# Two DVE operations for each weight tile, new planned durations and priorities in a fused attention and mixing kernel

## The chip, the cores and the metric

The kernel runs on one core of one Trainium2 chip. The metric is the device time of one execution in microseconds. Three runs of the kernel before took 783.48, 783.9 and 786.11 us (median 783.9).

The engines are named as in the profile: PE (TensorE, matmuls; PEld is its weight load), DVE (VectorE), ACT (ScalarE), POOL (GpSimd), SP (SyncE, whose queue issues all DMAs here). Each engine takes its instructions in order.

## The reference

Queries, keys and values have shape (4 batches, 8 heads, 576 positions, 64). Three steps follow each other:

```python
# 1. attention, the sum of two branches
q_d, k_d, v_d = means over groups of 4 positions          # 144 positions
out_up    = repeat(softmax(q_d k_d^T / 8) v_d, 4)
out_local = softmax(q k^T / 8 where |i - j| < 4) v
x = (out_up + out_local) as (4, 576, 512)
# 2. channel mixing with the row before
xk = mu_k * x + (1 - mu_k) * x_prev
xr = mu_r * x + (1 - mu_r) * x_prev
x  = sigmoid(xr @ w_r) * (relu(xk @ w_k)**2 @ w_v)
# 3. normalisation and a two-layer block
x  = x + relu(layernorm(x) * g_ln @ w_ch1) @ w_ch2
```

w_r is 512 x 512, w_k 512 x 1024, w_v 1024 x 512, w_ch1 512 x 2048, w_ch2 2048 x 512. These five weights arrive as 64-bit floats, everything else as 32-bit floats.

## The kernel before, in words

**Attention** is done in 16 units, one for each pair of heads and batch (units 0 to 3 are batch 0). A unit loads its keys, queries and values, brings keys and queries to a layout with the head dimension on partitions, forms the banded scores (`score`, L584) and the scores of the means (`dscore`, L614), takes both softmaxes on DVE and ACT, multiplies with the values (`upper` L678, `pvmm` L700) and adds the two branches into a 128-row slice of xT (L725). All four units of a batch are needed for one row block of step 2, because each gives 128 of the 512 channels.

**Forms of the loads.** The parameters m0 to m15 choose for each unit how keys and queries come in (`load`, L459): 0 is four DMAs for each tensor in 128-byte runs and a transpose on DVE (L525); 1 is two DMAs in 256-byte runs and six transposes on PE (L544); 2 is two DMAs in 1536-byte runs and twelve small matmuls with the identity on PE (L538); 3 loads as 1 does and multiplies with a matrix that also gives the sums over four positions (L541). In all forms but 0, ACT or DVE copies the result out of PSUM.

**Steps 2 and 3** run over six chunks of 384 rows. A product in 32-bit precision is three matmuls (`mm3`, L740 to L743): each operand is split into a high and a low part, and high x high, high x low and low x high are added up in PSUM. Step 3 does its first two chunks directly and the last four in pairs by a seven-product scheme (`m2_h`).

**Weights.** `load_split` (L396) takes each of 52 tiles of 128 x 512 weights (4 of w_r, 8 of w_k, 8 of w_v, 16 each of w_ch1 and w_ch2): a DMA of 64-bit words into w64 (two buffers), a conversion to 32-bit floats in wf (two buffers), a copy of the high part, a subtraction for the low part. The conversion (`load_f32`, L371 to L394) is one ACT operation, the absolute value of the high words read as 32-bit floats (L379), and four on DVE: a clamp from below (L382), a shift by 3 with a mask (L385), an OR with the low word's three top bits (L388) and an OR with the sign (L392).

**The order** is worked out by a planner in Python (`Plan`, L61). Every operation is added with an engine (or several to choose from), an assumed duration and a priority; the planner simulates the engines and takes, at each step, the operation that can start earliest, the lowest priority value first among those ready. Its sequence is what is issued, so it fixes the order on each in-order queue. Assumed durations come from `c_act`, `c_dve`, `c_pool` and `c_dma` (L241 to L254) and from constants; DMAs are one engine "SP" that is busy for the assumed transfer time, and their data is taken to land 2.2 us after it. Priorities come from the dictionary `PRM` (L26). `LOAD` adds a handicap to DVE where an operation has a choice.

**Filler.** 40 warm-up matmuls of 128 columns (`warm_up`, L415) go first, four or five ahead of each score of batch 0, and `issue` (L221) adds one for each 0.06 us in which the plan has PE idle, until PSUM bank pv2 is needed.

**Small loads.** mu_k, mu_r and g_ln (512 values each) are loaded into [128, 4] tiles, in 4-byte pieces (L340, L341, L1217).

## Time and profile before

| | |
|---|---|
| runs | 783.48, 783.9, 786.11 us |
| profiled execution, its own time | 791.19 us |
| its span | 789.4 us |
| mean granted TensorE clock | 0.982 |
| PE, PEld busy | 762.4 us (97%), 667.3 us (85%) |
| DVE, ACT, POOL busy | 531.6 us (67%), 374.3 us (47%), 116.1 us (15%) |
| moved by DMA | 120.31 MB in 187,199 packets |

The busy times are averages over stages with different limits, and a PE that is busy with filler counts as busy. In the rows below, a window's line gives for each engine the busy time and in brackets how many instructions ran; PEclk is the granted clock as a share of full speed. A wait's line names the instruction that waited, then what released it. "issue" is time in which an engine waited for nothing that the profile shows.

### The profile page before, as it was taken

The numbers are of one execution on the slowest core, as the hardware profiler recorded it, in microseconds if no ns is written. First come the engines' busy times: TensorE is split into PE (matmuls) and PEld (weight loads), VectorE is DVE, ScalarE is ACT, GpSimd is POOL, SyncE is SP. The second block draws the span as 40 slices with busy tenths as digits, with TensorE's granted clock in tenths as the row PEclk, the third lists the DMA queues.
The fourth block names the chain that finished last, engine by engine and source line by source line (L and its number), as shares of the span: only waits on it lengthen the run. The fifth ranks groups of instructions, "written<-read, shape, count | busy, mean of one in ns | idle before, by whom it ended". The sixth has DMA issues, their size and how long they took to land.

```text
span 789.4 us, 15623 instructions
## 1 busy us (share of the span) xinstructions
PE 762.4 (97%) x5940; PEld 667.3 (85%) x5940; DVE 531.6 (67%) x1094; ACT 374.3 (47%) x854; POOL 116.1 (15%) x162
## 2 busy tenths in 40 slices
PE   7798789999999999999999999999999999999998
PEld 7677667788788798888999999998988888898986
DVE  5799698974775768998889986737553355333233
ACT  4678676765865766858644334411421131111110
POOL 6332243312320100100001022200100030000000
PEclk9789898999999999999999999999999999999999
DMA  8899799453540033446475698887854346544422
GB/s 214 176 165 166 151 174 150 102 97 81 124 52 22 34 119 128 159 149 167 129 190 169 196 328 224 252 321 263 196 152 112 117 121 216 171 120 113 128 68 80
DMA packets 187199, 120.31 MB, mean 152 GB/s; under 512 B 129524, under 2 KB 154996, under 8 KB 187124
## 3 DMA queue, kind: packets, MB, share of 16 engines
q1 hardware_dynamic: 187124, 119.32, 58.8%
q8 instruction: 47, 0.77, 0.4%
q14 instruction: 28, 0.23, 0.1%
HBM read 90.44 MB, written 28.84 MB: 151 GB/s over the span
## 4 chain that ended last, share of the span: by engine, by line
PE 82%; DVE 7%; DMA 5%; ACT 3%; issue 2%; SPq 1%; DVEq 0%; ACTq 0%
PE pso L742 8%; PE pso L743 8%; PE pso L741 8%; PE psh L741 7%; PE psh L743 7%; PE psh L742 7%; PE psk L741 4%; PE psk L743 4%; PE psk L742 4%; PE psv L741 4%; PE psv L742 4%; PE psv L743 4%; PE pv L711 2%; DMA w<-in_moe_w_k_dram 2%; PE ds L619 2%
## 5 line engine op out<-in xcount | busy, mean ns | idle before, releaser
L741 PE MATMUL psh<-xn,sa 128*128 128x384 f32 x224 | 75.7, 338 | 1.8 <-ACT u L359 1.0
L743 PE MATMUL psh<-xn,sa 128*128 128x384 f32 x224 | 75.5, 337 | 0.0
L742 PE MATMUL psh<-xn,sa 128*128 128x384 f32 x224 | 75.3, 336 | 0.0
L741 PEld LDWEIGHTS psh<-xn,sa 128*128 128x128 f32 x224 | 42.1, 188 | 7.0 <-ACT u L359 1.4
L379 ACT ACTIVATE wf<-w 128x512 f32<-128x512 f32 x52 | 34.7, 668 | 27.1 <-DMA w<-in_moe_w_ch_dram 10.2
L742 PEld LDWEIGHTS psh<-xn,sa 128*128 128x128 f32 x224 | 42.1, 188 | 3.9
L743 PEld LDWEIGHTS psh<-xn,sa 128*128 128x128 f32 x224 | 42.1, 188 | 0.0
L367 ACT ACTIVATE c22h<-t 128x384 fp32r<-128x384 f32 x16 | 8.4, 525 | 66.2 <-DVE t L1136 66.2
L367 ACT ACTIVATE kr<-psk 128x384 f32<-128x384 f32 x46 | 22.5, 490 | 34.7 <-PE psk L743 29.0
L388 DVE SCALAR_TENSOR_TENSOR wf<-w,wf 128x512 uint32<-128x512 uint32 x52 | 37.0, 714 | 0.5
L392 DVE SCALAR_TENSOR_TENSOR wf<-w,wf 128x512 uint32<-128x512 uint32 x52 | 36.7, 707 | 0.4
L806 DVE TENSOR_TENSOR kl<-kr,kh 128x384 fp32r<-128x384 f32 x38 | 21.7, 570 | 20.3 <-ACT kr L805 20.1
L382 DVE TENSOR_SCALAR wf<-wf 128x512 f32<-128x512 f32 x52 | 24.1, 464 | 15.8 <-ACT wf L379 15.6
L367 ACT ACTIVATE hh<-psh 128x384 fp32r<-128x384 f32 x32 | 15.7, 489 | 35.9 <-PE psh L743 35.3
L417 PE MATMUL warm<-identb 128*128 128x128 bf16 x308 | 27.6, 244 | 3.9 <-issue 2.1
L572 POOL TENSOR_TENSOR v<-v 72x512 f32<-72x512 f32 x16 | 21.7, 1357 | 57.6 <-DMA v<-in_v_dram 50.0
L417 PEld LDWEIGHTS <-identb 128*128 128x128 bf16 x308 | 22.2, 111 | 5.3 <-issue 2.7
L363 ACT COPY PT<-pT 32x288 f32<-32x288 f32 x54 | 23.1, 428 | 6.8 <-PE pv L711 5.8
L367 ACT ACTIVATE c11h<-psh 128x384 fp32r<-128x384 f32 x16 | 7.9, 491 | 38.6 <-PE psh L743 38.5
L803 ACT ACTIVATE kh<-kr 128x384 fp32r<-128x384 f32 x48 | 25.1, 524 | 0.8
L1113 DVE SCALAR_TENSOR_TENSOR c11l<-psh,c11h 128x384 fp32r<-128x384 f32 x16 | 8.8, 553 | 24.4 <-ACT c11h L367 24.2
L854 POOL TENSOR_TENSOR raw<-raw 128x384 f32<-128x384 f32 x5 | 5.9, 1181 | 128.3 <-DVE xn L1081 67.7
(772 smaller groups left out, 2396.8 us busy)
## 6 DMA issues: line engine op xcount, KB each, us to landing
sa<-s_dram SPq DMA_DIRECT2D x112, 256.0 KB
w<-in_moe_w_ch_dram SPq DMA_DIRECT2D x32, 512.0 KB
s_dram<-s SPq DMA_DIRECT2D x16, 512.0 KB
vw<-in_v_dram SPq DMA_DIRECT2D x62, 96.0 KB
v<-in_v_dram SPq DMA_DIRECT2D x16, 288.0 KB
x_dram<-r SPq DMA_DIRECT2D x18, 256.0 KB
x1t<-x_dram SPq DMA_DIRECT2D x6, 768.0 KB
z_dram<-x1t SPq DMA_DIRECT2D x18, 256.0 KB
```

The lines of the kernel that those rows point to most:

```text
L363: return [("ACT", c_act(n), lambda: nc.scalar.copy(dst(), src()), False), ("DVE", c_dve(n, True), lambda: nc.vector.tensor_copy(dst(), src ...
L367: return [("ACT", c_act(n, True), lambda: nc.scalar.activation(dst(), src(), AF.Relu), False), ("DVE", c_dve(n), lambda: nc.vector.tensor_ ...
L379: add("ACT", c_act(512), prio, lambda: nc.scalar.activation(f(), w64().bitcast(F32)[:, :, 1], AF.Abs), r=[w64], w=[f])
L382: add("DVE", c_dve(512, True), prio, lambda: nc.vector.tensor_scalar_max(f(), f(), TINY), w=[f], port=True)
L388: lambda: nc.vector.scalar_tensor_tensor(fu(), w64()[:, :, 0], 29, fu(), op0=ALU.logical_shift_right, op1=ALU.bitwise_or),
L392: lambda: nc.vector.scalar_tensor_tensor(fu(), w64()[:, :, 1], 0xC0000000, fu(), op0=ALU.bitwise_and, op1=ALU.bitwise_or),
L417: nc.tensor.matmul(warm()[:, :P], identb, identb, start=True, stop=True)
L572: lambda: nc.gpsimd.tensor_tensor(v4()[:, :, 0:2, :], v4()[:, :, 0:2, :], v4()[:, :, 2:4, :], op=ALU.add),
L741: nc.tensor.matmul(ps, lh, rh, start=start, stop=False, skip_group_check=more)
L742: nc.tensor.matmul(ps, lh, rl, start=False, stop=False, skip_group_check=more)
L743: nc.tensor.matmul(ps, ll, rh, start=False, stop=stop, skip_group_check=more)
L803: add("ACT", c_act(C), prio, lambda: nc.scalar.activation(kh(), kr(), AF.Square), r=[kr], w=[kh])
```

## The change

The conversion of a weight tile keeps two DVE operations. The absolute value on ACT now also scales by 2^-112, which puts the exponent where the shift by 3 needs it, so that clamp and mask go; a second ACT operation takes the top byte of each low word and writes it, scaled to 0 to 7, as a 32-bit integer in place, so that the OR needs no shift of its own.

```diff
-            add("ACT", c_act(512), prio, lambda: nc.scalar.activation(f(), w64().bitcast(F32)[:, :, 1], AF.Abs),
-                r=[w64], w=[f])
+            add("ACT", c_act(512), prio, lambda: nc.scalar.activation(
+                f(), w64().bitcast(F32)[:, :, 1], AF.Abs, scale=2.0 ** -112), r=[w64], w=[f])
+            add("ACT", c_act(512), prio, lambda: nc.scalar.activation(
+                w64()[:, :, 0], w64().bitcast(U8).rearrange("p a (b c) -> p a b c", c=4)[:, :, 0, 3], AF.Copy,
+                scale=7.45 / 255), w=[w64])
             fu = lambda: f().bitcast(U32)
-            add("DVE", c_dve(512, True), prio, lambda: nc.vector.tensor_scalar_max(f(), f(), TINY), w=[f],
-                port=True)
-            add("DVE", c_dve(512, True), prio,
-                lambda: nc.vector.tensor_scalar(fu(), fu(), 3, 0x3FFFFFF8, op0=ALU.logical_shift_left,
-                                                op1=ALU.bitwise_and), w=[f], port=True)
             add("DVE", c_dve(512), prio,
-                lambda: nc.vector.scalar_tensor_tensor(fu(), w64()[:, :, 0], 29, fu(),
-                                                       op0=ALU.logical_shift_right, op1=ALU.bitwise_or),
+                lambda: nc.vector.scalar_tensor_tensor(fu(), fu(), 3, w64()[:, :, 0],
+                                                       op0=ALU.logical_shift_left, op1=ALU.bitwise_or),
                 r=[w64], w=[f], port=True)
```

The planner's durations are set anew, and its DMAs now take 0.47 us of SP each and then pass one shared queue:

```diff
 def c_act(n, psum=False, ap=0):
-    return (0.05 if psum else 0.093) + n / 1200 + 0.093 * ap
+    return (0.07 if psum else 0.113) + n / 1200 + 0.093 * ap
 def c_dve(n, fast=False):
-    return 0.066 + n / (1920 if fast else 960)
+    return 0.116 + n / (1920 if fast else 960)
 def c_pool(n):
-    return 0.1 + n * 0.0022
+    return 0.2 + n * 0.0028
-def c_dma(nbytes, small=False):
-    return max(0.41, nbytes / 360e3 * (2 if small else 1))
+def c_dma(nbytes, run=2048):
+    return nbytes / run * min(6.5 + run / 18, 20 + run / 26) / 16e3
...
+            if eng == "SP":
+                free[eng] = at + self.ISSUE
+                moved = max(moved, free[eng]) + cost
+                end = moved + o.lat
```

Constants of single operations change too (the copies into PT are costed as 420 elements instead of 288, `upper` 0.71 instead of 0.6, a matmul triple 3 x 0.0165 over its columns instead of 0.01). Nearly all values of `PRM` change: the handicap of DVE from 0.36 to 0.47; the priority base of w_r from -25.74 to -43.615 with a step for each tile of -56.938 instead of -0.4; the limit on thin matmuls in a row (`thin`) from 7.21 to 14.233; and the forms of the units:

```diff
-m0=2, m1=1, m2=1, m3=1, m4=3, m5=0, m6=1, m7=0, m8=0, m9=0
+m0=2, m1=1, m2=0, m3=3, m4=1, m5=0, m6=0, m7=2, m8=3, m9=0
```

Form 2 loads both heads of a tensor in one DMA instead of two. Filler is 304 columns wide, 17 ahead of all, two ahead of each score of batch 0, one for each 0.14 us of planned idle time:

```diff
-    def warm_up(n=40):
+    isumb = isum.bitcast(BF16)
+    def warm_up(n=17):
         for _ in range(n):
-            nc.tensor.matmul(warm()[:, :P], identb, identb, start=True, stop=True)
+            nc.tensor.matmul(warm()[:, :304], identb, isumb, start=True, stop=True)
...
-    plan.issue(lambda: warm_up(1), 0.06, pvs[0][2])
+    plan.issue(lambda: warm_up(1), 0.14, pvs[0][2])
```

mu_k, mu_r and g_ln are loaded together as rows of 512 bytes and transposed on PE:

```diff
-            add("SP", 0.9, PRM["mu"], load_mu, w=[mub], lat=2.2)
+            raw = Buf(wk, [P, C], F32, "kr", 1, "vraw")
+            for i, src in enumerate((mu_k, mu_r, g_ln)):
+                add("SP", 0.05, PRM["mu"], lambda i=i, src=src: nc.sync.dma_start(
+                    out=raw()[KT * i:KT * i + KT, :P], in_=src.rearrange("(k p) -> k p", p=P)), w=[(raw, i)], lat=2.2)
+            vps = Buf(ps_k, [P, 512], F32, "pk", 2, "vps")
+            add("PE", 0.1, PRM["mu"] + 8.0, lambda: nc.tensor.transpose(
+                vps()[:, :3 * KT], raw()[:3 * KT, :P], ident[:3 * KT, :3 * KT]), r=[raw], w=[vps])
+            add("ACT", c_act(12, True), PRM["mu"] + 8.0, lambda: nc.scalar.copy(vecs, vps()[:, :3 * KT]), r=[vps], w=[mub])
```

The sum of four value rows, two POOL operations before, becomes one step that the planner may give to POOL or, as a single reduction over 1,024 elements, to DVE; the scaling of the maxima by -1/128 may go to ACT instead of DVE.

## Rows read from the trace of the kernel before

**Rows 1.** Windows by stage: busy us and instructions of each engine, TensorE clock, DMA share, GB/s.
```profile
0.00:59.00 59.00, 49.10 (x937) 42.41 (x938) 44.81 (x96) 36.73 (x97) 27.01 (x52) 0.88 0.90 185
59.00:150.00 91.00, 80.17 (x1095) 64.68 (x1093) 79.26 (x169) 65.67 (x167) 27.55 (x39) 0.92 0.89 155
150.00:420.00 270.00, 269.38 (x2112) 234.67 (x2112) 213.33 (x460) 181.67 (x413) 37.01 (x51) 1.00 0.43 112
```

**Rows 2.** Groups by line, engine PE, first 60 us: busy us, mean ns, idle before.
```profile
L417 PE MATMUL warm<-identb 128*128 128x128 bf16 x297 | 25.1, 244 | 3.9 <-issue 2.1 <-DVE identb L318 1.8
```

**Rows 3.** Waits of PE, first 150 us: us in total, times, longest us.
```profile
PE up L681 <- ACT pdT L674: 3.7, 1, 3.7
PE sc L593 <- issue: 3.2, 2, 2.8
PE ds L619 <- DVE e L607: 2.5, 1, 2.5
PE warm L417 <- issue: 2.1, 1, 2.1
```

**Rows 4.** Windows of the four stretches behind those waits, columns as in rows 1.
```profile
22.30:26.50 4.20, 4.20 (x50) 3.50 (x50) 2.21 (x8) 1.05 (x3) 0.81 (x3) 0.50 1.03 198
...
37.80:43.50 5.70, 5.69 (x126) 4.29 (x126) 4.85 (x12) 3.18 (x10) 1.61 (x3) 0.50 1.05 154
...
89.60:95.50 5.90, 5.86 (x33) 4.63 (x34) 4.73 (x11) 3.33 (x8) 1.82 (x2) 0.50 0.70 208
...
119.30:126.50 7.20, 7.20 (x50) 5.42 (x51) 5.22 (x11) 3.69 (x12) 3.35 (x4) 0.53 0.78 128
```

**Rows 5.** DMA queues in the window from 17 to 24 us: packets, MB, share.
```profile
q1 hardware_dynamic: 3070, 1.61, 97.2%
q8 instruction: 1, 0.02, 1.1%
```

**Rows 6.** Chain of waits: start us, us, what; pieces between 28 and 109 us.
```profile
28.97 0.50 PE tq L544 x6
...
65.18 1.39 PE tq L541 x12
...
76.11 0.67 ACT wf L379
...
78.26 7.58 DMA w<-in_moe_w_k_dram
85.93 0.66 ACT wf L379
...
108.05 0.67 ACT wf L379
```

**Rows 7.** Groups by line, whole span: the conversion's operations (x52 weight tiles).
```profile
L379 ACT ACTIVATE wf<-w 128x512 f32<-128x512 f32 x52 | 34.7, 668 | 27.1 <-DMA w<-in_moe_w_ch_dram 10.2 <-DMA w<-in_moe_w_k_dram 8.2 <-DMA w<-in_moe_w_r_dram 6.5
...
L382 DVE TENSOR_SCALAR wf<-wf 128x512 f32<-128x512 f32 x52 | 24.1, 464 | 15.8 <-ACT wf L379 15.6
...
L385 DVE TENSOR_SCALAR wf<-wf 128x512 uint32<-128x512 uint32 x52 | 23.4, 452 | 0.3
```

**Rows 8.** Windows where the chain runs on DVE, lines L382, then L385: DVE busy us.
```profile
103.90:119.20 15.30, 1.62 (x2) 1.00 1.10 201
...
sum 40.80, DVE 2.45; mean DVE 0.82
...
103.90:119.20 15.30, 1.24 (x3) 1.00 1.10 201
...
sum 40.80, DVE 2.49; mean DVE 0.83
```

**Rows 9.** DMA in the window from 9 to 13.5 us: all packets.
```profile
DMA packets 2622, 0.95 MB, mean 211 GB/s; under 512 B 2493, under 2 KB 2493, under 8 KB 2621
```

**Rows 10.** Timeline of PE: start us, us; unit 0's transposes of keys and queries.
```profile
7.93 1.21 PE L538 MATMUL tq<-isum,kin 96*64 96x96 f32 x24
8.97 1.16 PE L538 MATMUL tq<-isum,qin 96*64 96x96 f32 x24
```

More of the change, by code (lines that the diff above doesn't have):

```diff
@@ L13 @@
 U32 = mybir.dt.uint32
+U8 = mybir.dt.uint8
 BF16 = mybir.dt.bfloat16
@@ L61 @@
 class Plan:
-    SYNC = {"PE": 0.2, "ACT": 0.15, "DVE": 0.14, "POOL": 0.16, "SP": 0.0, "CTL": 0.0}
+    SYNC = {"PE": 0.21, "ACT": 0.16, "DVE": 0.14, "POOL": 0.2, "SP": 0.0, "CTL": 0.0}
+    ISSUE = 0.47
     LOAD = {"PE": 0.0, "ACT": 0.0, "DVE": PRM["dve"], "POOL": PRM["pool"], "SP": 0.0, "CTL": 0.0}
@@ L146, in order @@
         thin = 0.0
+        moved = 0.0
         seq = []
@@ L194, in order @@
             seq.append(i)
+            end = at + cost + o.lat
             free[eng] = at + cost
+            if eng == "SP":
+                free[eng] = at + self.ISSUE
+                moved = max(moved, free[eng]) + cost
+                end = moved + o.lat
             if pt:
@@ L199, in order @@
                 thin = thin + cost if o.thin else 0.0
-            end = at + cost + o.lat
             for k in o.tiles:
@@ L331, in attn_moe_kernel @@
     keep(maskb[96:128, G - 1:G], -1, 27, 0)
-    muk = const.tile([P, KT], F32, name="muk")
-    mur = const.tile([P, KT], F32, name="mur")
-    gln = const.tile([P, KT], F32, name="gln")
-    omk = const.tile([P, KT], F32, name="omk")
-    omr = const.tile([P, KT], F32, name="omr")
-    def load_mu():
-        nc.sync.dma_start(out=muk, in_=mu_k.rearrange("(k p) -> p k", p=P))
-        nc.sync.dma_start(out=mur, in_=mu_r.rearrange("(k p) -> p k", p=P))
+    vecs = const.tile([P, 3 * KT], F32, name="vecs")
+    oms_ = const.tile([P, 2 * KT], F32, name="oms")
+    muk, mur, gln = (vecs[:, KT * i:KT * (i + 1)] for i in range(3))
+    omk, omr = oms_[:, :KT], oms_[:, KT:]
     PT = at.tile([P, 2, G, 96], F32, name="PT", bufs=1)
@@ L451, in hold @@
         def hold(n):
-            return 0.056 * n if first else 0.0
+            return 0.14 * n if first else 0.0
         mode = PRM[f"m{n}"]
@@ L460, in load @@
             if runs:
-                for hp in range(2):
-                    add("SP", c_dma(96 * 1536), early, lambda hp=hp: nc.sync.dma_start(
-                        out=dst()[:96, 384 * hp:384 * hp + 384],
-                        in_=src[b, 2 * u + hp].rearrange("(p c) d -> p (c d)", c=6),
-                    ), w=[(dst, hp)], lat=2.2)
+                add("SP", c_dma(192 * 1536, 1536), early, lambda: nc.sync.dma_start(
+                    out=dst()[:96].rearrange("p (h x) -> p h x", h=2),
+                    in_=src[b, 2 * u:2 * u + 2].rearrange("h (p c) d -> p h (c d)", c=6),
+                ), w=[dst], lat=2.2)
                 return
@@ L545, in tr @@
                                                 ident[:96, :96])
-                add("PE", (0.21 if runs else 0.21 if sums4 else 0.085) * m, pr(0.05), tr, r=[src], w=[tq])
+                add("PE", (0.12 if sums4 else 0.1) * m, pr(0.05), tr, r=[src], w=[tq])
                 if runs:
@@ L598, in score @@
                         )
-            add("PE", 0.9 + hold(4), pr(0.2), score, r=[qT, kT], w=[sc] + held, thin=True)
+            add("PE", 0.8 + hold(2), pr(0.2), score, r=[qT, kT], w=[sc] + held, thin=True)
             mx = Buf(at, [P, G, 1], F32, "mx", 2)
@@ L624, in dscore @@
                     )
-        add("PE", 0.9 + hold(5), pr(0.3), dscore, r=[qd, kd], w=[ds_] + held, thin=True)
+        add("PE", 1.0 + hold(2), pr(0.3), dscore, r=[qd, kd], w=[ds_] + held, thin=True)
         dsv = lambda: ds_()[:, :3 * SD].rearrange("p (t c) -> p t c", c=SD)
@@ L631, in attention @@
             lambda: nc.vector.tensor_reduce(mxd()[:, 0:3], dsv(), axis=AX.X, op=ALU.max), r=[ds_], w=[mxd])
-        add("DVE", c_dve(3), pr(0.35),
-            lambda: nc.vector.tensor_scalar_mul(mxd()[:, 0:3], mxd()[:, 0:3], -0.0078125), w=[mxd])
+        add([("DVE", 0.2, lambda: nc.vector.tensor_scalar_mul(mxd()[:, 0:3], mxd()[:, 0:3], -0.0078125), False),
+             ("ACT", 0.15, lambda: nc.scalar.mul(mxd()[:, 0:3], mxd()[:, 0:3], -0.0078125), False)],
+            0, pr(0.35), None, w=[mxd])
         for t in range(3):
-            add("ACT", c_act(SD, True, 2), pr(0.4),
+            add("ACT", 0.55, pr(0.4),
                 lambda t=t: nc.scalar.activation(pd()[:, t], dsv()[:, t], AF.Exp, bias=mxd()[:, t:t + 1],
@@ L1215, in attn_moe_kernel @@
     x1t, xn = {}, {}
-    glb = Fixed(gln)
-    add("SP", 0.45, T_2 - 30, lambda: nc.sync.dma_start(out=gln, in_=g_ln.rearrange("(k p) -> p k", p=P)),
-        w=[glb], lat=2.2)
+    glb = mub
     closed = [False]
```

84 lines of the change are left out of this document (40 added, 44 removed).

## The prediction

> **What bounds the kernel now.** Read the busy times by stage first [rows 1]. From 150 us to 420 us TensorE is busy for 269.4 of 270.0 us at the full granted clock, so nothing there can pay: an operation taken from another engine only widens slack that exists. The two stages before 150 us are different: TensorE is busy for 49.1 of 59 us and 80.2 of 91 us, at mean clocks of 0.88 and 0.92, while the DMA engines are busy for 0.90 and 0.89 of the time and VectorE (DVE) for 44.8 and 79.3 us. The first 60 us of busy time also hold 297 warm-up matmuls [rows 2], which compute nothing. So the loss sits in the first 150 us.
>
> Next, who TensorE (PE) waited for there [rows 3]: four idle times of 2 us or more, each with its own cause. One of 2.8 us ahead of the scores and one of 2.1 us ahead of a warm-up have no releaser that the profile shows ("issue"); one of 3.7 us waits for ScalarE (ACT), one of 2.5 us for DVE. Then look at the clock behind each of them [rows 4]: the stretches from 22.3, 37.8, 89.6 and 119.3 us ran at 0.50, 0.50, 0.50 and 0.53, the lower of the two levels (1.2 GHz of 2.4), each directly behind one of those idle times. A stretch at half clock gives back half its length: 2.1, 2.9, 3.0 and 3.4 us. Idle plus half clock makes four holes of 4.9, 5.0, 6.7 and 5.9 us, **22.5 us in all**. That is what the change can win, beside smaller idle times.
>
> What made the holes. During the first one the instruction queue moved one packet while the data queue held 97% of the DMA engines [rows 5]; I read the two "issue" holes as PE waiting for its own instructions behind that traffic. The third hole is a chain [rows 6]: a weight tile issued at 78.26 us lands 7.58 us later, ACT stands at the conversion of that tile until 85.93, and the copies queued behind it on ACT are what PE waits for. The fourth lies at the end of a stretch, 103.9 to 119.2 us, in which the chain of waits runs mostly on DVE.
>
> **The change part by part.** The sum is made against the profiled execution: its span is 789.4 us and its time 791.2 us, 7.3 us above the median of the three runs shown (783.9). I subtract the same amount from both.
>
> **Conversion on DVE.** Each of the 52 weight tiles loses the clamp and the shift-and-mask, 464 and 452 ns [rows 7], 0.92 us together; 20 tiles (w_r, w_k, w_v) are converted in the first 150 us, so at most 18.3 us of DVE time goes there, and at least nothing if DVE merely idles instead. On the chain: in the stretch that ends in the fourth hole the two operations take 1.62 + 1.24 = 2.86 us [rows 8], more than the 2.5 us that PE idles. I take that hole whole, its half clock too: **−5.9**. In all three stretches where the chain runs on DVE they take 2.45 + 2.49 = 4.94 us, so 2.08 us outside that one: **−2.1**. The other 32 tiles lie behind 260 us, under a full PE: nothing, unless PE stops being full there.
>
> **Conversion on ACT.** Each tile gains a copy of one byte in eight into 32-bit words. No row shows that form. The nearest is the absolute value of the same tile, read at the same stride, 668 ns [rows 7]; I take that, for nothing excludes a slower or faster one. Its cost is between nothing and 20 x 0.668 = 13.4 us. The chain passes through ACT's step of a weight tile three times between 59 and 150 us [rows 6], and there the copy stands between the absolute value and everything queued on ACT: 3 x 0.668, **+2.0**. The first DVE operation of a tile now waits for two steps of ACT, 0.668 later; with 0.92 us of DVE gone the tile is still done, and its buffer free for SP's next weight load, 0.25 us sooner, and behind the waiting operation on DVE stand the softmax steps that the fourth hole waits for. If ACT's cover goes (it idles 22.3 us in the first stage and 25.3 in the second [rows 1]), the whole 13.4 shows: a rival below.
>
> The Trainium skill, ScalarE: Activation LUTs, section Rules for kernel authors, says the opposite of this part: simple arithmetic belongs on VectorE and not on ScalarE. By that page the sum would keep a third DVE operation and no copy on ACT. The trace agrees on one operation, where 464 ns on DVE stand against 668 on ACT, but not on the engine: it is DVE that is nearly full where PE waits [rows 1].
>
> **Warm-up and filler.** 304 columns for each instruction instead of 128, so the same time is filled with 128/304 of the instructions: 297 matmuls become about 125, and with a weight load each, 344 of the 937 + 938 instructions that PE executes in the first 59 us [rows 1] go, about a fifth. The two "issue" holes are worth 9.9 us; fewer instructions reach the same point with fewer fetches, but four fifths of them stay and the DMA engines stay full. Between nothing and 9.9 I take half: **−5.0**. Coarser filler can hold a ready operation up by at most one matmul; filler is put only where the plan has PE idle, so I price that at nothing.
>
> **Planned durations and priorities.** They change only the order on each in-order queue; no instruction gets shorter. The third hole comes from an order in which ACT stands for a transfer that the plan believed landed. The new plan counts transfers into one shared queue and adds to nearly every DVE, ACT and POOL duration, so ACT should meet that tile later. But its price for a weight tile (512 KB in 4096-byte runs) is 1.42 us against 1.46 before, while the row shows 7.58 from issue to landing. Between nothing and 6.7 I take half: **−3.3**. That a new order opens another hole is possible everywhere before 150 us; it is in the range, not in the sum.
>
> **Vectors mu and g.** Three loads of 512 four-byte pieces become three of four 512-byte rows, one transpose and one ACT copy of 12 elements. In the window in which the first two were issued, 2,622 packets passed 16 engines in 4.5 us [rows 9], so 27 ns each on one engine; 1,024 fewer are 1.7 us of DMA time ahead of the second head pair's queries: **−1.7**, or nothing if those aren't awaited. g's 512 come at a time when they delay nothing visible. PE's queue gains a wait, that transpose for the three rows: behind it stand the scores of the first pairs, and were the rows late, all would be. The plan sets it 8 us behind the loads, so I price it at nothing; the cover is that filler is issued ahead of it.
>
> **Queries and keys.** Units 2 and 6 go from 256-byte to 128-byte runs (DVE transposes), 3 and 4 swap forms, unit 7 goes from 128 to 1536 bytes and unit 8 from 128 to 256, both with transposes on PE. Two units gain DVE transposes and two lose them: nothing. On DMA that is 2 x 2,304 packets more and 4,224 + 2,304 fewer, 1,920 fewer in all, at 27 ns over 16 engines 3.2 us less; all of it comes while other loads are ahead of need, so I price it at nothing, with a gain of 3.2 as the bound. SP's queue gets four entries fewer (8 more for units 2 and 6, 12 fewer for 0, 7 and 8). On PE the forms cost [rows 6, 10]: 24 matmuls in 1.04 us for one of the two tensors in unit 0's form, so 2.1 for unit 7; 1.39 for one tensor in the summing form, so 2.8 for unit 8; 0.50 for one in the plain form, so 1.0 saved in unit 6 (unit 2's lie where PE has filler). Units 7 and 8 run where PE is nearly full: **+3.9**.
>
> **The sum of v** may now go to DVE. Its one DVE operation reads 1,024 elements, twice a conversion's; at half the speed per element of the clamp [rows 7] that is 4 x 0.464 = 1.9 us a unit, for eight units 15, less than the 18.3 freed. The planner takes it only where DVE is free in its plan: nothing.
>
> Sum: −5.9 −2.1 +2.0 −5.0 −3.3 −1.7 +3.9 = **−12.1 us**; 791.2 becomes 779.1, the median 783.9 becomes **about 772**.
>
> **Rivals.** (a) *ACT becomes the engine PE waits for.* In the third hole PE already waits for ACT, and each copy adds 0.668 us ahead of whatever stands behind it. If the third and fourth holes stay and every one of the 20 copies shows, the sum is +13.4 +3.9 −5.0 −1.7 −2.1 = +8.5, **792 us**. It decides from eight copies on the path (8 x 0.668 = 5.3 against 4.9 of remaining gains). For it: the 3.7 us wait; against it: ACT idles 47 us in the first 150. (b) *The transfers hide it.* The DMA engines are busy for 0.9 of the first 150 us [rows 1]; if each stage ends when its weights land, a faster conversion only waits longer, only the vectors' 1.7 us remain, and the order's shifts cancel: **782 us**, no change. This is also the case in which the new durations, nearly equal to the old for a weight tile, do not do what they say. Against it: in the second half of the window the chain runs on DVE and ACT, not on transfers. (c) *All four holes close*: −22.5 −2.1 −1.7, and nothing for ACT or the forms: −26.3, **758 us**.
>
> **How the numbers follow.** Forecast 0.55, (a) 0.16, (b) 0.11, (c) 0.18. About 0.3% (781.5 to 786.3 us) is what a measurement can tell from no change. The forecast's own spread hardly reaches into it, so faster is 0.73, same 0.11, slower 0.16. The range starts at (c)'s own value less a little, and ends at 788: it takes in (b) and orders that lose what they win, and leaves out most of (a) and the far half of (c): 757 to 788.
>
> **What would show it.** Right: by the changed kernel's windows, none or one of the four half-clock stretches is left before 150 us; DVE's total falls by about 47 us and ACT's rises by about 35; TensorE's rows behind 150 us start some 12 us earlier and look the same. The copy's row is near 668 ns; a far longer one would make (a). "Issue" idle times of 2 us that remain would strike the 5.0; a weight landing that ACT still waits 3 us for would strike the 3.3. Holes opening behind 150 us, under what is now a full PE, would make the forecast wrong in a way that no term here covers.

## The result, and the profile after

The changed kernel takes 792.38 us (median of five runs, 789.44 to 798.33) where the kernel before takes 784.82 (five runs): a ratio of 1.0114, 95% interval 1.0065 to 1.0162. It is **slower by 1.1%**; the forecast was 772 and the range ended at 788. The profiled execution is the longest of the five, with a span of 796.5 us.

First the windows by stage, columns as in [rows 1]:

```profile
0.00:59.00 59.00, 51.24 (x735) 36.61 (x737) 35.89 (x70) 34.21 (x88) 15.34 (x43) 0.83 0.89 182
59.00:150.00 91.00, 84.84 (x974) 67.87 (x973) 79.84 (x154) 74.70 (x192) 17.13 (x22) 0.94 0.63 137
150.00:420.00 270.00, 266.40 (x2311) 229.56 (x2310) 204.90 (x412) 198.29 (x457) 20.91 (x39) 1.00 0.46 116
```

PE idles less before 150 us than before the change, 13.9 us against 20.7 (150 less the two PE times), and is yet further behind: its first dense matmul of step 2 starts at 68.1 us, where it started at 59.1, and it runs 2,311 instructions between 150 and 420 us, where it ran 2,112, because attention matmuls are left over (768 of the score matmuls, before 576). There it now idles 3.6 us, before 0.6, and 3.7 behind 420 us, before 5.7. Over the whole span PE idles 21.2 us (before 27.0) and is busy for 12.9 us more, of which 6.5 are filler and 6.7 transposes of keys and queries. The clock of the first stage fell from 0.88 to 0.83. DVE lost 8.9 us in the first stage and nothing in the second.

The lower clock is this execution's and not the kernel's: over the five runs the mean clock is 0.981 (this one) to 0.993, median 0.989. Over the runs of the kernel before that were timed beside the experiments the median is 0.987.

Then the waits of PE in the first 150 us [rows 3], and the windows at half clock behind them [rows 4]:

```profile
PE tq L545 <- DMA qin<-in_q_dram: 3.1, 1, 3.1
PE tq L548 <- ACT pd L644: 2.6, 1, 2.6
PE ds L626 <- DVE qd L572: 2.4, 1, 2.4
...
PE tq L542 <- ACT kT L360: 1.7, 1, 1.7
...
PE tq L542 <- issue: 0.7, 1, 0.7
```
```profile
22.80:26.30 3.50, 3.50 (x60) 2.28 (x60) 2.01 (x6) 2.37 (x6) 1.26 (x1) 0.52 0.62 111
33.30:50.00 16.70, 16.69 (x175) 12.59 (x176) 8.57 (x17) 8.76 (x28) 0.40 (x3) 0.50 0.74 157
83.20:88.00 4.80, 4.79 (x22) 3.80 (x23) 4.80 (x11) 3.46 (x7) 0.00 (x0) 0.64 1.14 175
127.60:135.00 7.40, 7.40 (x91) 5.50 (x91) 3.90 (x8) 4.24 (x13) 0.28 (x1) 0.56 0.51 83
```

Again four holes, with other waits ahead of them. The second stands out: behind a wait of 3.1 us PE runs 16.7 us at 1.2 GHz, although it is busy all the time. (In another execution of the same order it isn't there: see the sum of v below.)

The groups that answer to [rows 2, 7], whole span:

```profile
L422 PE MATMUL warm<-isum,identb 128*128 128x304 bf16 x187 | 34.0, 332 | 2.0 <-DVE identb L323 1.8 <-issue 0.3
L386 ACT ACTIVATE w<-w 128x512 uint32<-128x512 uint8 x52 | 34.8, 668 | 0.0
L391 DVE SCALAR_TENSOR_TENSOR wf<-wf,w 128x512 uint32<-128x512 uint32 x52 | 35.6, 685 | 14.6 <-ACT w L386 14.2
L581 DVE TENSOR_REDUCE vd<-v 72x256 f32<-72x1024 f32 x14 | 28.0, 2004 | 10.3 <-DMA v<-in_v_dram 6.1 <-PE up L689 4.1
```

The copy on ACT costs 668 ns, as priced; the DVE operation behind it waits for it for 14.2 us in all. ACT's total rose by 28 us (374.3 to 402.7). DVE's fell by 16 us (531.6 to 515.5), not by 47: 14 of the 16 sums of v went to DVE, 28.0 us.

The chain of waits (start, us, what) leads into the first two holes:

```profile
16.10 5.60 DMA w<-in_moe_w_k_dram
21.70 0.02 issue
21.73 0.66 ACT wf L384
22.39 0.37 ACT pd L644 x2
22.76 0.04 issue
22.80 0.60 PE tq L548 x2
...
26.75 6.42 DMA qin<-in_q_dram
33.17 0.14 issue
33.31 2.03 PE tq L545 x8
```

ACT stands for a weight tile that lands 5.60 us after its issue, where the plan books 4.1 (0.47 for SP, 1.42 for the transfer, 2.2 for landing) when its queue is empty, with softmax steps queued behind it: the picture of [rows 6], some 60 us earlier. The second hole is a late load of unit 3's queries. SP's queue shows why it is late (start, us, line, what, how many), the changed kernel first:

```profile
9.98 2.97 SPq L502 DMA_DIRECT2D vw<-in_v_dram  x4
13.90 0.35 SPq L378 DMA_DIRECT2D w<-in_moe_w_r_dram  x1
...
16.55 0.94 SPq L502 DMA_DIRECT2D vw<-in_v_dram  x2
17.59 5.49 SPq L481 DMA_DIRECT2D kin<-in_k_dram  x4
...
26.29 1.38 SPq L473 DMA_DIRECT2D qin<-in_q_dram  x2
```
```profile
24.06 2.15 SPq L469 DMA_DIRECT2D qin<-in_q_dram  x2
26.26 1.02 SPq L498 DMA_DIRECT2D vw<-in_v_dram  x2
```

Before, the value windows (vw) go out from 26.26 us on, behind the keys and queries of units 2 and 3. In the changed kernel eight of them go out ahead of all of these, and a ninth ahead of unit 3's. The four loads of unit 2's keys then hold SP for 5.49 us, where the new plan books 4 x 0.47.

### The profile page after: what moved, and what is told of

The parts are those of the page before. It is cut to its first block, busy times and chain, and to the rows that moved or that the text cites. A ratio compares the mean times of both kernels' runs of the same rounds, so it can differ in the third digit from the quotient of the medians.

```text
span 796.5 us, 15410 instructions
## 1 busy us (share of the span) xinstructions
PE 775.3 (97%) x5868; PEld 669.2 (84%) x5868; DVE 515.5 (65%) x999; ACT 402.7 (51%) x925; POOL 75.3 (9%) x121
## 4 chain that ended last, share of the span: by engine, by line
PE 81%; DVE 8%; DMA 5%; ACT 4%; issue 1%; SPq 0%; POOL 0%; DVEq 0%; POOLq 0%; ACTq 0%
PE pso L750 8%; PE pso L751 8%; PE pso L749 8%; PE psh L749 8%; PE psh L751 8%; PE psh L750 8%; PE psk L749 4%; PE psk L751 3%; PE psk L750 3%; PE psv L749 3%; PE psv L751 3%; PE psv L750 3%; PE warm L422 2%; DMA v<-in_v_dram 2%; DVE vd L581 1%; PE sc L600 1%
## 5 line engine op out<-in xcount | busy, mean ns | idle before, releaser
L391 DVE SCALAR_TENSOR_TENSOR wf<-wf,w 128x512 uint32<-128x512 uint32 x52 | 35.6, 685 | 14.6 <-ACT w L386 14.2
L368 ACT ACTIVATE hh<-psh 128x384 fp32r<-128x384 f32 x32 | 15.7, 491 | 48.6 <-PE psh L751 44.9
L395 DVE SCALAR_TENSOR_TENSOR wf<-w,wf 128x512 uint32<-128x512 uint32 x52 | 35.7, 689 | 0.7
L422 PE MATMUL warm<-isum,identb 128*128 128x304 bf16 x187 | 34.0, 332 | 2.0 <-DVE identb L323 1.8
L386 ACT ACTIVATE w<-w 128x512 uint32<-128x512 uint8 x52 | 34.8, 668 | 0.0
L581 DVE TENSOR_REDUCE vd<-v 72x256 f32<-72x1024 f32 x14 | 28.0, 2004 | 10.3 <-DMA v<-in_v_dram 6.1
L967 DVE SCALAR_TENSOR_TENSOR hl<-psh,hh 128x384 fp32r<-128x384 f32 x32 | 17.7, 553 | 24.3 <-ACT hh L368 24.2
L814 DVE TENSOR_TENSOR kl<-kr,kh 128x384 fp32r<-128x384 f32 x43 | 24.2, 564 | 13.9 <-ACT kr L813 11.8
L773 DVE SCALAR_TENSOR_TENSOR tmu<-xT,oms,tmu 128x384 f32<-128x384 f32 (+1 forms) x64 | 31.1, 517 | 1.5 <-ACT tmu L767 1.4
L767 ACT ACTIVATE tmu<-xT,vecs 128x192 f32<-128x192 f32 (+1 forms) x54 | 26.1, 521 | 6.5 <-DVE xrl L777 2.7
L422 PEld LDWEIGHTS <-identb 128*128 128x128 bf16 x187 | 19.0, 109 | 11.6 <-issue 2.3
```

What stands on the lines that cost most here:

```text
L368: return [("ACT", c_act(n, True), lambda: nc.scalar.activation(dst(), src(), AF.Relu), False), ("DVE", c_dve(n), lambda: nc.vector.tensor_ ...
L386: add("ACT", c_act(512), prio, lambda: nc.scalar.activation(w64()[:, :, 0], w64().bitcast(U8).rearrange("p a (b c) -> p a b c", c=4)[:, :, ...
L391: lambda: nc.vector.scalar_tensor_tensor(fu(), fu(), 3, w64()[:, :, 0], op0=ALU.logical_shift_left, op1=ALU.bitwise_or),
L395: lambda: nc.vector.scalar_tensor_tensor(fu(), w64()[:, :, 1], 0x80000000, fu(), op0=ALU.bitwise_and, op1=ALU.bitwise_or),
L422: nc.tensor.matmul(warm()[:, :304], identb, isumb, start=True, stop=True)
L581: ("DVE", c_dve(1024), lambda: nc.vector.tensor_reduce(vd(), v4().rearrange("p a r d -> p a d r"), axis=AX.X, op=ALU.add), False)],
```

## The experiments

Every ratio is to the kernel before, timed beside it on the same chip; its median there was 785.6 to 787.0 us. The experiments ran on four chips, so two kernels are compared by their ratios, with both intervals. "Frozen" means that the order on PE and SP is unchanged but for the edit named (filler aside where its width changes); "planned anew" means that the planner ran again with the edit.

**Conversion and order, taken apart.** Two frozen kernels cross the two: the new conversion in before's order, and the old one in the changed order. Each emits the other's operations at the old places.

```diff
 # in before's order: the clamp's place takes the copy, the mask's nothing
-            nc.vector.tensor_scalar_max(f(), f(), TINY)
+            nc.scalar.activation(w64()[:, :, 0], <top byte of the low word>, AF.Copy, scale=7.45 / 255)
-            nc.vector.tensor_scalar(fu(), fu(), 3, 0x3FFFFFF8, ...)
 # in the changed order: the reverse
```

> The kernel before with the new conversion alone, every queue in the order of before (the byte copy stands on ACT where the clamp stood on DVE). Theory A (the new order of loads and work is what costs; the conversion is innocent): 778 to 786 us, equal or a little faster than before. Theory B (the copy on ACT, 0.668 us a tile, is what PE ends up waiting for): 788 to 793 us. Theory C (the sums of v on DVE, 2.0 us each, are what costs): 778 to 786 us, as A.

Measured 1.0035 (1.0012 to 1.0057), 787.7 us: in the gap between the two ranges, and a little slower than before.

> The changed kernel with the conversion of before (one ACT and four DVE operations) at the same places of the same order. Theory B: 782 to 788 us. Theories A and C: 792 to 800 us, equal or slower than the changed kernel, because DVE gets 47 us more to do in an order planned without them.

Measured 1.0238 (1.0208 to 1.0268), 803.7 us, above the 800 that any theory allowed. So the loss is in the order and what goes with it, but its size depends on the conversion. With the old conversion the new order costs 2.4%; with the new one it costs 0.8% (1.0035 to 1.0114). The 2.4% is not the order's price alone, because that order was planned with 47 us less on DVE. In the changed order the new conversion is worth 1.2% (1.0238 to 1.0114). In before's order it gives nothing, although DVE's work fell as forecast, by 6.7 us in each of the first two stages:

```profile
0.00:59.00 59.00, 48.78 (x936) 42.05 (x937) 38.07 (x81) 40.48 (x105) 26.83 (x52) 0.88 0.99 187
59.00:150.00 91.00, 81.34 (x1108) 65.38 (x1107) 72.61 (x151) 73.09 (x185) 27.74 (x41) 0.96 0.87 157
```

DVE merely idles longer; the DMA engines are at 0.99 in the first stage. With the old conversion in the changed order PE waits behind 150 us, too: waits of PE, 150 to 430 us, where the changed kernel's ACT waits are 1.3 and 0.8 us.

```profile
PE psk L753 <- ACT r L797: 3.5, 2, 2.0
PE psr L753 <- ACT r L797: 1.3, 2, 0.7
```

**The sum of v** back on POOL, frozen.

```diff
-             ("DVE", c_dve(1024), lambda: nc.vector.tensor_reduce(...), False)]
+             ("DVE", c_dve(1024), vsum, False)]
```

> The changed kernel with the 14 sums of v that stand on DVE done on POOL at the same places of the same order. Theory C (28 us of DVE time, 2.0 us each against 1.18 planned, hold up the softmax steps): 782 to 787 us. Theories A and B: 789 to 795 us, as the changed kernel.

Measured 1.0108 (1.0072 to 1.0145): the same. The 28 us on DVE cost nothing that can be measured. SP's queue is the changed kernel's, with the values early, and yet the long stretch at half clock is not in this execution: PE does not wait for unit 3's queries, and the window from 33.3 to 50 us runs at full clock. (It has a stretch of 6.8 us at half clock from 23.2 us on, behind a wait of 3.8 us for ACT.)

```profile
33.30:50.00 16.70, 16.59 (x343) 12.67 (x342) 13.69 (x28) 14.09 (x42) 5.17 (x10) 1.00 1.01 206
```

**The old priorities** (with before's forms), planned anew.

```diff
-PRM = dict(thin=14.233, t0=0.033, ...
+PRM = dict(thin=7.21, t0=4.89, ...
```

> The changed kernel with the whole parameter dictionary of before (priorities, forms of the units, handicap of DVE); the planner's new durations, its new account of transfers and all else stay. Theory A splits: if the priorities and forms cost the time, 776 to 785 us; if the planner's new account of transfers does (values of unit 0 issued early, ahead of later queries), 788 to 796 us. Theories B and C: 788 to 796 us.

Measured 1.0209 (1.0179 to 1.0238), 802.0 us: slower than either branch. Putting the old priorities back is no cure; whether the new ones cost time in the change is not shown by it, since the whole order is another.

**The account of transfers**, both ways, planned anew: the old one in the changed kernel, the new one in the kernel before.

```diff
-            if eng == "SP":
-                free[eng] = at + self.ISSUE
-                moved = max(moved, free[eng]) + cost
-                end = moved + o.lat
```

> The changed kernel with the planner's account of transfers put back: a DMA holds SP for its whole assumed time, at the old prices; everything else is the change's, and the order is planned anew. Theory A1 (the account of 0.47 us of SP for each DMA and one shared queue behind it lets unit 0's values and weight tiles out ahead of the keys and queries of units 2 and 3): 785 us or less, the first half-clock stretch behind 33 us gone, the first step-2 matmul near 59 us instead of 68. Theory A2 (the engines' new durations or the unit forms make the loss): 790 or more, with the stretch from 33 to 50 us at half clock still there.

Measured 1.0218 (1.0185 to 1.0251).

> The kernel before with the new account of transfers and the new transfer prices alone, planned anew. A1: 790 us or more, with a new half-clock stretch ahead of 60 us. A2: within 0.4% of before (782 to 789).

Measured 1.0238 (1.0202 to 1.0274). Slower both ways, so this pair names no cause. A1's time came, but not its half-clock stretch: the first 59 us of this kernel ran whole at full clock. Planned anew with a part exchanged, three kernels lose 2.1 to 2.4%. That suits priorities and account being fitted to each other; it does not show it, for another order may lose by itself.

**The old forms of the units**, planned anew.

```diff
-m2=0, m3=3, m4=1, ... m6=0, m7=2, m8=3
+m2=1, m3=1, m4=3, ... m6=1, m7=0, m8=0
```

> The changed kernel with before's forms of the units (m0 to m8), all else the change's, planned anew: units 2 and 3 load in 256-byte runs again, and SP then issues unit 1's and 2's keys and queries ahead of unit 0's last values. A1: 790 us or more, since the account is still the new one. A3 (the 128-byte runs of unit 2, issued behind the values, are what unit 1 to 3 wait for): 785 or less, the stretch behind 33 us shorter by half or more.

Measured 1.0080 (1.0049 to 1.0110), 793.5 us: A1's time, 0.3% under the changed kernel and inside its interval. Its profile has A3's sign, with the window from 35 to 40 us at full clock, and the time did not follow.

**Wide filler** in before's order, frozen, with the new conversion and with the old.

```diff
-            nc.tensor.matmul(warm()[:, :P], identb, identb, start=True, stop=True)
+            nc.tensor.matmul(warm()[:, :304], identb, isumb, start=True, stop=True)
```

> Before's order with the new conversion (as in the first experiment, 1.0035 of before) and with 304-column filler in place of 128 columns, each for the same planned time; the order of all other instructions is before's. If the two idle times without a releaser come of too many instructions on the busy DMA engines: both fall below 1 us, and the time falls by 5 us or more against the conversion alone, to 780 to 783. If wide filler only hid them in the changed order: they stay near 2.8 and 2.1 us, and the time is 786 to 789.

Measured 0.9985 (0.9961 to 1.0008), 785.4 us: between the two ranges. Against the conversion alone (1.0035) that is 0.5% less, and the intervals do not meet.

> Before's order and before's conversion with the 304-column filler alone. If the wide filler is what gained 4 us behind the conversion alone, and the conversion gives nothing in this order: 781 to 784 us, as before or 0.3 to 0.5% under it. If the conversion pays once the fetch holes are smaller: 787 or more, slower than the conversion with wide filler (0.9985 of before).

Measured 0.9984 (0.9958 to 1.0009): with wide filler, too, the conversion gives nothing in this order. The idle time without a releaser is not gone either. The timeline's line of the first of the two, and its DMA queues from 37.7 to 41.7 us:

```profile
41.74 0.37 PE L597 MATMUL sc<-kT,qT 64*32 64x32 f32 x9 [4.01 <-issue]
```
```profile
q1 hardware_dynamic: 1810, 0.47, 108.1%
q8 instruction: 1, 0.02, 2.2%
```

PE stops for 4.01 us in the middle of a group of 48 like matmuls; in that time one packet passes the instruction queue q8, among 1,810 of data. By the trace's packet records it has 16,384 bytes and ends at 40.17 us, 1.57 us before PE goes on. In the two "issue" holes before the change that lag is 1.53 and 1.50 us. The kept traces have 18 such stops of 1 us or more in the first 150 us, and in 16 of them PE goes on 1.4 to 1.7 us behind the end of a packet on q8 (in the other two 2.3 and 2.9). That bears out the reading of these holes as late instructions, by the lag and not by a test. The four profiles of before's order with narrow filler have 1.5 to 5.9 us in such stops, the four with wide filler 1.1 to 4.0.

The profiles also settle the fourth hole. Four have before's order and the old conversion: the kernel before in both its executions, wide filler alone, and the values early (below). In all four PE waits 2.3 to 3.0 us for DVE ahead of `ds` at 113 to 119 us, and the 6.4 to 7.2 us behind it run at 0.50 to 0.54. Four have the new conversion in before's order: by itself, with wide filler, and with wide filler less the copy or with the rows of mu (both below). There that wait is 0.8 to 1.4 us, with full clock behind it. But then PE waits 1.7 to 2.4 us for ACT, at 117 to 132 us, and the 4.6 to 5.7 us behind that run at 0.63 to 0.70. The timeline shows it, with the idle time and its releaser in brackets, for wide filler alone and then, in two lines, for the conversion with wide filler:

```profile
115.41 1.42 PE L621 MATMUL ds<-kd,qd 64*64 64x144 f32 x12 [2.98 <-DVE e L609]
```
```profile
112.84 0.95 PE L623 MATMUL ds<-kd,qd 64*64 64x144 f32 x12 [1.36 <-DVE e L611]
...
129.44 0.47 PE L685 MATMUL up<-pdT,vd 72*64 72x144 f32 x4 [1.78 <-ACT pdT L678]
```

The conversion does close the hole it was meant to close, and another wait, for ACT, comes behind it.

**The conversion without the copy on ACT**, same kernel, frozen.

```diff
-nc.vector.scalar_tensor_tensor(fu(), fu(), 3, w64()[:, :, 0], ...
+nc.vector.scalar_tensor_tensor(fu(), fu(), 3, <zero>, ...
```

> The conversion with wide filler in before's order, less the second ACT operation: the low word's three top bits are left out (a zero is ORed in), so each tile takes one ACT and two DVE operations. If the copy on ACT is what eats the gain of the conversion (my +2.0 was too small; the third theory of the first call): 3 us or more below the conversion with wide filler, 0.9945 of before or less. If transfers set the end of the first 60 us, where the DMA engines are 97 to 103% busy: the same within 0.2%, 0.9965 to 1.0005.

Measured 0.9968 (0.9940 to 0.9996): 0.17% below, 1.3 us, inside the intervals. In before's order the copy is not what eats the gain: the new wait for ACT is there without it, 2.2 us at 127.6.

**Filler in the changed order**, frozen: gap filler stopped, or halved, behind the 109th.

```diff
-    plan.issue(lambda: warm_up(1), 0.14, pvs[0][2])
+    plan.issue(lambda: warm_up(1) if filled[0] < 109 else None, 0.14, pvs[0][2])
```

> The changed kernel with its order, but no filler in planned gaps behind the 109th warm-up matmul (46 us in its trace); the pairs ahead of the scores stay, 117 warm-ups in place of 187. In the trace of the changed kernel PE does not idle at all between 45 and 83 us but for 0.7 us, and runs some 15 us of filler there. Theory F (PE is behind its plan there after the half-clock stretch, and the filler, which an in-order queue cannot skip, stands ahead of work that is ready): 780 to 786 us, 6 to 12 less than the change, with the first step-2 matmul at 60 us or before. Theory G (PE's operands are not there, the filler fills real waiting): 791 us or more, idle time in its place, and half clock behind it.

Measured 1.0089 (1.0055 to 1.0122).

> The same with every second gap filler behind the 109th left in (152 warm-ups). F: about half of the gain, 786 to 789 us. G: 791 or more; if the filler left is enough to hold the clock, the same as the change, 791 to 793.

Measured 1.0077 (1.0045 to 1.0108). Theory F falls. Without the filler PE waits where the filler stood, as the waits of the first kernel show (first 150 us):

```profile
PE up L692 <- ACT pdT L685: 3.3, 2, 2.3
PE pv L722 <- ACT PT L364: 2.9, 2, 1.6
...
PE pv L722 <- DVE e L617: 1.8, 1, 1.8
```

**The value windows of units 0 and 1**, frozen: nine entries of SP's queue moved, nothing else. In the changed kernel behind units 2's and 3's keys and queries, in the kernel before ahead of unit 2's.

```diff
+        late = [i for i in seq if self.ops[i].mark in (("vw", 0), ("vw", 1))]
+        seq = rest + late + seq[to + 1:]
```

> The changed kernel with nothing moved but nine DMAs on SP: the value windows of units 0 and 1 go out behind the keys and queries of units 2 and 3 instead of ahead of them; all other queues keep their order. In the changed kernel's trace they take SP and the DMA engines from 10 to 17.5 us, and PE uses the first of them at 42.8 us. Theory K (they hold up the loads that PE waits for at 33 us, and the 16.7 us at half clock follow from that): 784 to 788 us, PE's wait for qin at 33 us under 1.5 us or some 4 us earlier, the half-clock stretch at least halved. Theory L (PE waits there for whatever lands last: the DMA engines are full either way, and the values are then missing later): 790 us or more, with waits for vw in the first 60 us.

Measured 1.0057 (1.0039 to 1.0076).

> The kernel before with the same nine DMAs moved the other way, ahead of unit 2's keys, where the change has them; nothing else. K: 4 to 8 us slower than before, 1.005 to 1.010. L: within 0.3% of before.

Measured 1.0031 (1.0007 to 1.0054). Both go the way of theory K, by less than it said: 0.57% won where they go late, 0.31% lost where they go early. By their times, 790.6 us and 0.31%, both lie at the edge of theory L; L's wait for vw is not in the first kernel's first 60 us. The loss is just clear of no change (1.0007), the gain is not clear of the changed kernel (1.0065 against 1.0076). The trace does not decide either. PE's wait for qin at 33 us is gone from the first kernel, but it is gone from the kernel with the sums on POOL as well, where the values are early. What is left is one stretch at half clock, 10.5 us for 16.7:

```profile
39.50:50.00 10.50, 9.86 (x148) 6.40 (x148) 9.41 (x18) 8.12 (x25) 1.60 (x4) 0.51 0.99 197
```

> The changed kernel with before's forms of the units (1.008 before) and the value windows of units 0 and 1 late as well. K and the forms together: 0.995 to 1.002 of before, 781 to 787 us. L: 1.006 to 1.010.

Measured 1.0065 (1.0034 to 1.0095): the forms add nothing to it that can be measured.

**The conversion known to before's planner** (wide filler; all else before's), planned anew, with the two DVE operations out of the plan and the copy in it.

```diff
+            add("ACT", c_act(512), prio, <the copy>, w=[w64])
-            add("DVE", c_dve(512, True), prio, <clamp>, w=[f], port=True)
-            add("DVE", c_dve(512, True), prio, <shift and mask>, w=[f], port=True)
```

> The kernel before with the wide filler and with the new conversion known to its planner (durations, priorities, forms and transfer account are before's), so that the order is planned anew around the shorter conversion. If an order fitted to the freed DVE is what the conversion needs: 778 to 783 us, 0.990 to 0.996. If any new order with priorities not fitted to it loses, as three re-planned kernels did (1.021 to 1.024): 795 or more.

Measured 1.0107 (1.0077 to 1.0138), 793.3 us: between the two expectations, and as slow as the changed kernel, without its durations, priorities, forms or account. Its first 150 us ran at full clock and its first dense matmul came at 51.5 us, 7.6 earlier than before the change. What it lost lies behind 150 us, mostly in waits for ACT. Its windows, then that of the kernel with the old priorities:

```profile
59.00:150.00 91.00, 81.27 (x1192) 64.22 (x1188) 83.27 (x175) 72.28 (x188) 33.88 (x51) 1.00 0.80 152
150.00:420.00 270.00, 263.84 (x1961) 228.90 (x1962) 188.55 (x393) 188.76 (x415) 32.80 (x41) 0.98 0.43 112
```
```profile
150.00:420.00 270.00, 258.05 (x2049) 222.64 (x2048) 202.17 (x399) 188.48 (x436) 19.66 (x35) 0.99 0.42 107
```

From 150 us to its end PE idles 12.1 us in this profile, 12.7 to 15.7 in the three with priorities or account exchanged and 13.1 in the changed order with the old conversion. In the eight profiles of before's order it is 5.9 to 7.9, in the changed kernel 7.3. So these orders lose behind 150 us, and the changed kernel does not.

**Rows of mu** in the frozen kernel with conversion and wide filler.

```diff
-        nc.sync.dma_start(out=muk, in_=mu_k.rearrange("(k p) -> p k", p=P))
+            nc.sync.dma_start(out=raw[0][KT * i:KT * i + KT, :P], in_=src.rearrange("(k p) -> k p", p=P))
+                nc.tensor.transpose(warm()[:, 504:512], raw[0][:2 * KT, :P], ident[:2 * KT, :2 * KT])
```

> The conversion with wide filler in before's order (0.9985 of before), with mu_k and mu_r loaded as rows of 512 bytes and transposed on PE as the change does, in the same place: 1,024 four-byte packets fewer while the DMA engines are full, the nearest thing to a version that beats both kernels. By my term of -1.7 us: 0.996 to 0.997 of before, 783 us. If the transfers behind them are not awaited: 0.998 to 0.999.

Measured 0.9959 (0.9935 to 0.9983), 782.34 us: **faster than both kernels**. It is 0.26% (2.0 us) under the same kernel without the rows (0.9985), which was timed on another chip; the two intervals overlap. Whether the conversion is needed in it was not tried.

**The kernel before, again.**

> The kernel before once more, unchanged, for a second profiled execution. If the four holes on which the prediction rests (22.5 us, in an execution 7.3 us above the median) belong to the kernel: again four half-clock stretches before 150 us and a mean clock near 0.98. If a part of them belongs to that one execution: holes at other places, 15 us or less of them, a mean clock of 0.99, and a ratio of 1.000 within its interval.

Measured 1.0003 (0.9980 to 1.0026). Its second profiled execution has a span of 784.0 us, 5.4 less. Its waits of PE in the first 150 us, and those three of its windows of 5 us that ran whole at half clock:

```profile
PE pv L711 <- DMA vw<-in_v_dram: 4.4, 1, 4.4
PE pv L711 <- ACT PT L363: 2.5, 2, 1.4
PE ds L619 <- DVE e L607: 2.3, 1, 2.3
PE sc L593 <- issue: 1.9, 2, 1.5
PE up L681 <- ACT pdT L674: 1.9, 2, 1.2
```
```profile
15.00:20.00 5.00, 5.00 (x40) 4.38 (x39) 2.83 (x7) 2.90 (x7) 1.83 (x3) 0.50 0.97 256
...
40.00:45.00 5.00, 3.98 (x35) 3.48 (x35) 2.71 (x6) 1.69 (x5) 1.34 (x3) 0.51 0.87 127
...
115.00:120.00 5.00, 5.00 (x39) 3.65 (x35) 3.77 (x7) 3.00 (x10) 3.35 (x4) 0.50 0.59 151
```

Of the four waits of [rows 3] only that of `ds` for DVE is there again at 2 us or more, with half clock behind it, some 6 us earlier. The largest is one that [rows 3] do not have, for a load of values; it stands ahead of the half-clock stretch near 40 us, where before a wait without a releaser stood. The stop in the middle of the scores came at 13 us and not at 19, and the stretch from 89.6 us on is gone.

## Why the prediction was wrong

**The step that failed: "That a new order opens another hole is possible everywhere before 150 us; it is in the range, not in the sum."** I gave the new durations and priorities a gain only (-3.3). Taken apart along before's order, the sum missed by 21 us: the conversion there was forecast at -6.0 (-5.9, -2.1 and +2.0) and came out at +2.7 (1.0035), and all that goes with the new order at -6.1 and came out at +6.2 (1.0035 to 1.0114). With the old conversion the same order costs 18.7 us. The order's loss had no place in the sum. In the changed kernel's profile it is there at 150 us already, with dense work 9 us late, and it is in PE's busy time (12.9 us more, filler and transposes) and not in its idle time (5.8 less). Neither of the two is the cause by itself: without the transposes, and without the filler, PE waits instead, and the time moved by less than the intervals. For other new orders "before 150 us" was also too narrow; four of them idle 5 us or more longer behind it than the kernel before.

Rival (a) said 792, and 792 it is, but its mechanism is not what the runs show, so the number is luck. It adds 13.4 us for copies on ACT, and in before's order leaving the copy out gains 1.3 us, inside the intervals. In the changed order, where DVE waits for the copy for 14.2 us, it was not left out by itself; what it costs there is open.

How much of the order is traced: the nine value loads go 0.57% one way and 0.31% the other, only the second clear of no change, and no trace shows by which wait. The old forms, the filler and the sums of v each moved the time by less than the intervals. At least half of the 1.1% is **open**. Priorities and transfer account can't be split by exchanging one, because each kernel planned anew with one exchanged lost 2% or more, and a kernel planned anew for nothing but the conversion lost 1.1%; the engines' new durations by themselves were not tried. That ACT stands for a weight tile at 21.7 us is seen in the trace; moving that conversion alone was not tried.

**"I take that hole whole" (-5.9), and the other DVE time (-2.1).** The fourth hole did close, in all four profiles with the new conversion in before's order, and the time stayed (1.0035; with wide filler 0.9985 against 0.9984 without the conversion). What failed is the step from a closed hole to a shorter time: a wait for ACT opened behind it. I also read the holes of one execution as pieces that add up; of the four, the second execution has one gone, one 6 us earlier, one behind another wait and one as it was. That a later resource takes over is the picture of rival (b), for before's order, but not with the transfers of the first stage alone: the first dense matmul comes at 57.3 us with wide filler alone, at 58.7 with the conversion as well and at 54.0 with the copy left out, and the three times are within 0.2%. Which transfer or engine sets the end was not isolated. In the changed order, which was planned with the short conversion, the same conversion is worth 1.2%, part of it behind 150 us, where I had written that nothing can pay: PE idles there for 13.1 us with the old conversion and 7.3 with the new.

**Conversion on ACT (+2.0).** The price of one was right to the nanosecond (668). Leaving it out gave 1.3 us, inside the intervals. The Trainium skill's rule that such arithmetic belongs on VectorE (ScalarE: Activation LUTs, section Rules for kernel authors) is neither borne out nor refuted: the copy was left out, not moved to DVE.

**Warm-up and filler (-5.0; "coarser filler ... nothing").** In the changed kernel the two "issue" idle times are gone (0.7 and 0.3 us), as the step said. But this is not the wide filler's doing alone: in before's order one of 4.0 us is left. Wide filler is worth 0.16% with the old conversion, inside its interval, and 0.5%, 3.9 us, with the new one, so the half that I took is not ruled out. The filler's total rose from 27.6 to 34.0 us, and that costs nothing that can be measured: stopped, it leaves idle time.

**Planned durations (-3.3).** I named its own weakness, the price of 1.42 us for a weight tile, and still took half. (I set it against 7.58 us from issue to landing; the plan adds 2.2 us of landing to it, so it was short by less than that.) ACT waits for such a tile again (2.15 us up to 21.73).

**Vectors (-1.7).** The 2.0 us between two kernels on two chips fit it, but are inside the intervals. Its price is too high: 27 ns is the mean of all packets in that window. By their records, the 4-byte packets of the first 60 us before the change took 12 ns each, so 1,024 of them come to 0.8 us.

**Forms (+3.9).** Transposes of keys and queries take 17.8 us of PE's first 150, before 11.7, partly at half clock; undoing them gave 0.3%, 2.7 us, inside the interval. That fits the size, and with the values late as well nothing shows that it adds to the rest.

**The sum of v.** I put one at 1.9 us and it took 2.0. The planner gave DVE 14 of 16 of them, one of them at 80.4 us right ahead of the wait for DVE in the third hole, though with all of them on POOL the time was the same.

**What was left out of the range:** it ended at 788, with no room for what the order could lose. A new order should have had a term of its own, of either sign and of the size of the holes.

## What to carry to other kernels

A hole in one profiled execution belongs to that execution until a second profile shows it again. A hole that does come again can be closed and the time still stay: here its last releaser was made faster, and the wait went to the next one. Before a new order is costed, write SP's queue out for both plans and look which loads move past which, and don't take the stage that is full now to stay full: four of the new orders lost 5 us or more there. The version that beats both kernels keeps before's order whole and takes from the change only the conversion, the wide filler and the rows of mu_k and mu_r.

## What the runs showed of the hardware

An issue on SP is not of one length. Four DMAs in 128-byte runs held SP for 5.49 us from 17.59 us on, 1.4 each, with the DMA engines at 0.90; the next two in the same form took 0.98 together, with the engines at 0.40. In the same execution the three loads of mu_k, mu_r and g_ln, four rows of 512 bytes each, took 0.64, 0.29 and 0.29, with the engines full, so a full set of engines by itself does not make an issue long.

PE can stand still for 4.01 us within a run of like matmuls while data fills the DMA queues at 108%. That its own instructions are late is inferred from the packets on the instruction queue, but by a lag that comes again: in 16 of 18 such stops PE goes on 1.4 to 1.7 us behind the end of one. The Trainium skill, Runtime: NRT & Kernel Launch, section Instruction fetch mechanics, says that this fetch is mostly hidden behind the issue of instructions; if these 4 us are fetch, they were not.

A reduction on DVE over 1,024 elements read at a stride of 64 took 2,004 ns, while an operation on two tensors of 512 took 685: 2.0 ns for each element read by the one, 0.7 by the other.
